# Seven products for one more channel matmul, features moved to ScalarE and an earlier load

One core of one Trainium2 chip runs the whole program. The metric is the device time of one execution in microseconds (us). All runs compared below are fast, at a granted TensorE clock of 0.99 to 1.00 (0.985 to 0.991 in e4), unless a sentence says otherwise. "The kernel before" and "the changed kernel" are the two kernels; batch b's attention and token mixing run inside the channel MLP of an earlier batch.

## The reference

```python
def phi(x, c, s):                     # c, s: cos and sin of pi/2 * position / 576
    r = np.maximum(x, 0.0)
    return np.concatenate([r * c, r * s], axis=-1)
q_p, k_p = phi(q, cos_w, sin_w), phi(k, cos_w, sin_w)      # q, k, v: 8 x 8 x 576 x 64
kv  = np.einsum('bhsf,bhsd->bhfd', k_p, v)
num = np.einsum('bhsf,bhfd->bhsd', q_p, kv)
den = np.einsum('bhsf,bhf->bhs', q_p, k_p.sum(axis=2))[..., None] + 1e-06
x = (num / den)                       # -> 8 x 576 x 512
h = np.maximum(x.T @ w_tok1, 0.0) @ w_tok2                 # token mixing, per batch
u = x + h.T
out = u + np.maximum(u @ w_ch1, 0.0) @ w_ch2               # channel MLP, 512 -> 1536 -> 512
```

## The kernel before

The program is a list of groups. Group g does the channel MLP of batch g in 12 steps of the first matmul and then the second matmul; each step also carries pieces of two later batches: numerators and token mixing of batch g+1 (`b` below), features, query transposes and KV sums of batch g+2 (`f`). From group 2 on the second matmul is done in seven products (a Strassen scheme: sums of the left operand on VectorE, seven quarter products on TensorE, sums of the results on VectorE and GpSimd). Group 1 is still the plain product, because its helpers had not found room.

Names used below: `h1T` is the relu of the first channel matmul, `B` the relu between the two token-mixing matmuls, `qpT` the transposed query features and `uT` the transposed u. A batch has 576 = 4.5 x 128 rows; its last 64 are its tail, and the tails of two batches are worked on together.

```python
def mlp2(g, t, part, ps, sub=(0, 4)):            # plain: 48 matmuls of 512 columns in group 1
    for ki in range(4 * part + sub[0], 4 * part + sub[1]):
        nc.tensor.matmul(ps, h1T[:, ki, t * P:(t + 1) * P], wc2[:, ki, :],
                         start=(ki == 0), stop=(ki == NCH - 1))
# ... in the seven-product form: 14 units of six matmuls of 256 columns
#     (products in order: A11*B11, S2*T2, S3*T3, S1*T1, A12*B21, A22*T4, S4*B22)

if g == 1:                                        # what group 1 carries, by step
    put(19, tail_turn, 1)                         # transpose of two batches' tail rows
    # ... KV and numerators of batch 2
    for j in range(NJ):
        put(8 + j, f1k, f, j, 1, A)               # batch 3: sine feature of k on ScalarE
        put(10 + j, f1k, f, j, 0, V)              #          cosine feature on VectorE
        put(8 + j, vcast, f, j, G)                #          cast of v on GpSimd
        put(18 + j, kv_step, f, j)
    for j, at in enumerate((12, 15, 16, 17, 18)):
        put(at, q_step, f, j)                     # q: cosine on VectorE, sine on ScalarE,
                                                  # then a DMA transpose qp -> qpT
    for i in range(4):
        put(19 + i, t_sum, i)                     # sums of the second weight
    put(8, v_load, 4); put(20, q_load, 4); put(22, k_load, 4)
# ... groups 2 to 6:
for j in range(NJ):
    put(2 + j, num_step, b, j)                    # numerators read qpT: group 2 reads batch 3's
```

In the groups shown here all loads and all DMA transposes are issued from SyncE, in program order; the outputs are stored from GpSimd. The loads of batch 3 (k, v, q) stood behind the five query transposes of batch 2.

## Time and profile before

The median was 262.94 us of 3 runs (262.86 to 263.52), the profiled span 261.9 us.

| stage | length, us | what TensorE waited for in it, us |
|---|---|---|
| group 1 (plain product) | 29.23 | 0.16 for a feature of k |
| group 2 | 27.78 | 0.34 and 0.27 for relus of h1T on ScalarE; 0.15 at its end for a transposed u |
| group 3 | 26.03 | none over 0.12 |
| groups 4 and 5 | 26.50, 25.86 | none over 0.12 |

A stage runs from the first matmul of one group to that of the next, so whatever delays it in between is in its length. The table is worked out from the starts of the groups' first matmuls (58.10, 87.33, 115.11, 141.14, 167.64 and 193.50 us). Groups 2 and 4 have the same instructions, so 26.50 us is what group 2 takes when nothing waits. One view that the prediction does not show matters later: TensorE in the middle of group 2, where it reads the transposed queries. (Columns of a timeline: start, length, engine, line, operation, out<-in, shape, count, and in brackets the idle time before it with what ended it.)

```profile
93.24 0.41 PE L207 MATMUL psA<-kv_sb,qpT 128*128 128x65 bf16 x8
94.35 0.41 PE L207 MATMUL psA<-kv_sb,qpT 128*128 128x65 bf16 x8
```

These are the fourth and fifth numerators of batch 3. No bracket: their transposes had landed at 90.14 and 91.43 us, 3.1 and 2.9 us early.

### The profile page before, as it was taken

The numbers are of one execution on the slowest core, as the hardware profiler recorded it, in microseconds if no ns is written. First come the engines' busy times: TensorE is split into PE (matmuls) and PEld (weight loads), VectorE is DVE, ScalarE is ACT, GpSimd is POOL, SyncE is SP. The second block draws the span as 40 slices with busy tenths as digits, with TensorE's granted clock in tenths as the row PEclk, the third lists the DMA queues.
The fourth block names the chain that finished last, engine by engine and source line by source line (L and its number), as shares of the span: only waits on it lengthen the run. The fifth ranks groups of instructions, "written<-read, shape, count | busy, mean of one in ns | idle before, by whom it ended". The sixth has DMA issues, their size and how long they took to land.

```text
span 261.9 us, 5595 instructions
## 1 busy us (share of the span) xinstructions
PE 250.9 (96%) x2060; PEld 154.4 (59%) x2074; DVE 187.2 (71%) x447; ACT 148.3 (57%) x246; POOL 97.9 (37%) x175
## 2 busy tenths in 40 slices
PE   7788999999999999999999999999999999999994
PEld 2465455554545554775587557755875576486483
DVE  5794657697959688948993999489939773563563
ACT  4664486785577438836792679367935452613610
POOL 5178465361042420292029402830291045045041
PEclk9999999999999999999999999999999999999999
DMA  6999999999987999989999997995381034003004
GB/s 188 356 371 388 391 388 387 326 180 267 379 270 159 251 298 357 221 188 305 361 193 179 323 343 151 185 290 99 65 215 70 3 80 161 19 3 150 13 0 161
DMA packets 79947, 57.18 MB, mean 218 GB/s; under 512 B 48176, under 2 KB 74928, under 8 KB 79920
## 3 DMA queue, kind: packets, MB, share of 16 engines
q1 hardware_dynamic: 76128, 47.26, 67.5%
q0 software_dynamic: 2560, 8.39, 9.3%
q10 hardware_dynamic: 1232, 1.18, 1.4%
q8 instruction: 16, 0.26, 0.4%
q14 instruction: 11, 0.09, 0.1%
HBM read 35.85 MB, written 9.44 MB: 173 GB/s over the span
## 4 chain that ended last, share of the span: by engine, by line
PE 54%; DMA 1%; ACT 1%; DVE 1%; issue 1%
PE psM L312 24%; PE psM L374 21%; PE psA L232 3%; PE psA L250 3%; PE psA L207 2%; PE psA L183 1%; DMA uT<-u_bf 1%; PE psA L374 1%; ACT kp L138 0%; PE psA L291 0%; ACT u_bt L299 0%; DVE res L397 0%; DVE res L423 0%; DVE qp L140 0%; DVE kp L140 0%
## 5 line engine op out<-in xcount | busy, mean ns | idle before, releaser
L312 PE MATMUL psM<-uT,w_ch 128*128 128x512 bf16 x368 | 88.0, 379 | 0.2
L324 ACT ACTIVATE h1T<-psM 128x512 bf16<-128x512 f32 x93 | 55.4, 597 | 42.3 <-PE psM L312 40.4
L312 PEld LDWEIGHTS <-w_ch 128*128 128x128 bf16 x416 | 38.1, 97 | 40.4 <-issue 0.4
L392 POOL TENSOR_TENSOR res<-res,u_sb 128x256 f32<-128x256 f32 x36 | 26.7, 772 | 78.2 <-DVE res L397 77.8
L156 POOL CAST vb<-v_raw 128x512 bf16<-128x512 f32 (+1 forms) x43 | 23.4, 589 | 25.2 <-DMA v_raw<-in_v_dram 12.3
L138 ACT ACTIVATE kp<-k_raw,sin_t 128x512 bf16<-128x512 f32 (+1 forms) x45 | 28.1, 666 | 1.2 <-DMA k_raw<-in_k_dram 1.2
L138 ACT ACTIVATE qp<-q_raw,sin_t 128x512 bf16<-128x512 f32 (+1 forms) x40 | 26.3, 681 | 4.4 <-DMA q_raw<-in_q_dram 4.4
L374 PEld LDWEIGHTS <-h1T 128*128 128x128 bf16 x252 | 23.8, 98 | 6.2 <-issue 0.6
L374 PEld LDWEIGHTS <-k_raw 128*128 128x128 bf16 x252 | 24.4, 98 | 5.1 <-issue 1.2
L330 PE MATMUL psM<-w_ch,h1T 128*128 128x512 bf16 x92 | 23.3, 379 | 0.2
L374 PE MATMUL psM<-w_ch,h1T 128*128 128x256 bf16 x168 | 22.3, 273 | 0.6 <-ACT h1T L324 0.6
L140 DVE TENSOR_SCALAR kp<-k_raw,cos_t 128x512 bf16<-128x512 f32 (+1 forms) x45 | 19.7, 465 | 1.8 <-DMA k_raw<-in_k_dram 1.8
L207 PEld LDWEIGHTS <-qpT 128*128 128x128 bf16 x320 | 14.9, 98 | 9.9 <-issue 1.8
L374 PE MATMUL psM<-w_ch_t,k_raw 128*128 128x256 bf16 x162 | 20.5, 273 | 0.0
L140 DVE TENSOR_SCALAR qp<-q_raw,cos_t 128x512 bf16<-128x512 f32 (+1 forms) x40 | 16.6, 447 | 5.4 <-DMA q_raw<-in_q_dram 5.2
L255 DVE TENSOR_TENSOR u_sb<-psA,x_sb 128x1024 f32<-128x1024 f32 x16 | 19.5, 1216 | 1.0 <-PE psA L250 0.8
L223 DVE TENSOR_TENSOR x_sb<-psA,rden 128x512 bf16<-128x512 f32 x28 | 19.4, 691 | 1.0
L354 DVE TENSOR_TENSOR k_raw<-h1T 128x512 bf16<-128x512 bf16 (+1 forms) x28 | 9.9, 353 | 11.8 <-ACT h1T L324 11.1
L250 PE MATMUL psA<-B,w_tok 128*128 128x512 bf16 x64 | 16.4, 379 | 0.0
L440 POOL DMA_DIRECT2D out_dram<-res x16 | 9.0, 560 | 18.6 <-DVE res L335 12.8
L219 DVE TENSOR_SCALAR rden<-psA 128x8 f32<-128x8 f32 x35 | 5.7, 163 | 13.4 <-PE psA L207 13.1
L193 ACT CAST kv_sb<-psA 128x520 bf16<-128x520 f32 x7 | 4.2, 603 | 18.9 <-PE psA L183 18.9
(134 smaller groups left out, 377.4 us busy)
## 6 DMA issues: line engine op xcount, KB each, us to landing
out_dram<-res POOLq DMA_DIRECT2D x32, 256.0 KB, 3.8
k_raw<-in_k_dram SPq DMA_DIRECT2D x7, 640.0 KB, 8.8
v_raw<-in_v_dram SPq DMA_DIRECT2D x7, 640.0 KB, 10.5
q_raw<-in_q_dram SPq DMA_DIRECT2D x7, 640.0 KB, 10.9
k_raw<-in_k_dram SPq DMA_DIRECT2D x7, 512.0 KB, 7.1
v_raw<-in_v_dram SPq DMA_DIRECT2D x7, 512.0 KB, 10.4
q_raw<-in_q_dram SPq DMA_DIRECT2D x7, 512.0 KB, 10.1
u_sb<-in_moe_w_ch_dram SPq DMA_DIRECT2D x2, 1024.0 KB, 10.6
```

Of the source, the lines that this page charges most:

```text
L138: eng.activation(out_ap, in_ap, AF.Relu, bias=0.0, scale=s)
L140: eng.tensor_scalar(out_ap, in_ap, scalar1=s, scalar2=0.0, op0=ALU.mult, op1=ALU.max)
L156: eng.tensor_copy(out_ap, in_ap)
L207: nc.tensor.matmul(dst, w, kv_sb[:, h, 0:E1], start=True, stop=True, skip_group_check=True)
L223: nc.vector.tensor_mul(dst.rearrange("p (g h d) -> p g h d", g=2, h=HH), n[:, :, :, 0:D], rb)
L250: nc.tensor.matmul(ps[:, half, :], w2[:, ki, 2 * c + half, :], B1[b % 2][:, ki, :], start=(ki == 0), stop=(ki == NT - 1))
L255: nc.vector.tensor_add(u_sb[b % 2][:, 2 * c:2 * c + 2, :], ps, x_sb[:, 2 * c:2 * c + 2, :])
L312: nc.tensor.matmul(ps.rearrange("p (t k) -> p t k", k=P), wc1[:, ki, mi * P:(mi + 1) * P], src[:, :, ki, :], start=(ki == 0), stop=(ki == ...
L324: eng.activation(h1T[:, mi, :], ps, AF.Relu)
L330: nc.tensor.matmul(ps, h1T[:, ki, t * P:(t + 1) * P], wc2[:, ki, :], start=(ki == 0), stop=(ki == NCH - 1))
L374: nc.tensor.matmul(m[tt][:, tt, :], a[:, c, tt * P:(tt + 1) * P], w[:, c, :], start=(pr < 4 and c == 0 and (tt == 0 or own)), stop=(c == N ...
L392: G.tensor_add(c[:, t, :], s[:, t, :], u[:, t, :])
```

## The change

Its intent: give group 1 the seven-product form as well (less TensorE work), and make room on VectorE by moving features of batch 3 to ScalarE. The values of batch 3 are loaded ahead of its keys, the weight sums are spread over group 1, and three of the four sums of group 1 live in the raw buffers of batch 2 (one of them in its q buffer, into which q of batch 4 is loaded later), since those of batch 3 are still in use.

```diff
+    S_of = {1: (rows_of(raw["k"][0], 0), rows_of(raw["k"][0], 1), rows_of(raw["q"][0], 0), S4_sb)}
@@ between the second and third query transpose of batch 2
+    load(3, v, "v", (SY, SY))
     for j in range(2, NJ):
         qfeat(2, j, A, A)
         qturn_dma(2, j)
+    for n in "kq":
+        load(3, src_of[n], n, (SY, SY))
@@ later
-    for n in "kvq":
-        load(3, src_of[n], n, (SY, SY))
@@ group 1's plan
+            for i, at in enumerate((4, 12, 17)):
+                put(at, t_sum, (1, 3, 2)[i])
+            put(10, s_sums, g, 0, 3)
+            put(11, s_sums, g, 3, 5)
-                put(8 + j, f1k, f, j, 1, A)
-                put(10 + j, f1k, f, j, 0, V)
-            for j, at in enumerate((12, 15, 16, 17, 18)):
-                put(at, q_step, f, j)
+                put((9, 10, 10, 11, 11)[j], f1k, f, j, 1, A)
+                put((12, 13, 18, 20, 21)[j], qfeat, f, j, (A, A, A, A, V)[j], A)
+                put((12, 13, 18, 20, 21)[j], qturn_dma, f, j)
+                put((15, 15, 17, 18, 19)[j], f1k, f, j, 0, (A, A, A, V, V)[j])
+                put(5, vcast, f, j, G)
-            put(20, q_load, 4)
+            put(22, q_load, 4)
@@ later groups
-            put(0, q_load, f + 1)
+            put(8 if g == 2 else 0, q_load, f + 1)
@@ the loop over the steps
-            elif g == 1:            # plain product
-                ...
-                mlp2(g, t, part, mps[t])
             else:
                 mlp2_unit(g, s - NCH)
                 mlp2_sums(g, s - NCH)
```

Cut: buffer views, arguments, the order of the first matmul's blocks in group 1, the first weight sum ahead of group 1, the lines that the new ones for `vcast`, `t_sum` and `kv_step` replace, and the transposes of u, which move two steps later in group 1.

## The prediction

> **What bounds the kernel now.** I read the page's busy shares and 40 slices first, then the chain of waits, then a table of windows with one stage per row, then the timelines of the engines inside the two stages that the change touches. Group g is batch g's channel MLP (g = 8: the tails of all batches); one stage is one group's first matmul (L312) and second matmul (L330, or L374 for the seven-product form), with the next batches' attention and token mixing woven in.
>
> ```profile
> PE 250.9 (96%) x2060; PEld 154.4 (59%) x2074; DVE 187.2 (71%) x447; ACT 148.3 (57%) x246; POOL 97.9 (37%) x175
> PE   7788999999999999999999999999999999999994
> PEclk9999999999999999999999999999999999999999
> ```
>
> TensorE is busy 250.9 of 261.9 us at the full granted clock. Only 11 us are idle, and slices 1 to 4 and the last, the head and the final store, hold most of them. So time comes off almost only by taking TensorE work away, or from the little idle time of a middle stage.
>
> ```profile
> 218.95 10.36 PE psM L312 x48
> 229.31 9.17 PE psM L374 x84
> ```
>
> These two lines of the chain of waits, near its end, give the real price of each kind of matmul where nothing disturbs it: 48 of 512 columns take 10.36 us, so 215.8 ns each; 84 of 256 columns take 9.17 us, so 109.2 ns each. (The groups' means of 379 and 273 ns contain the overlapping drains and must not be multiplied.)
>
> ```profile
> 58.10:87.33 29.23, 28.91 (x236) 14.75 (x238) 23.73 (x45) 17.27 (x29) 6.06 (x11) 1.00 0.92 266
> 87.33:115.11 27.78, 26.96 (x235) 17.14 (x235) 22.28 (x53) 16.48 (x28) 9.57 (x15) 1.00 1.12 269
> 115.11:141.14 26.03, 25.96 (x230) 17.18 (x232) 20.47 (x51) 16.69 (x27) 9.40 (x16) 1.00 1.11 258
> 141.14:167.81 26.67, 26.62 (x234) 17.26 (x236) 21.56 (x52) 17.26 (x28) 11.20 (x18) 1.00 1.02 249
> ```
>
> The windows are groups 1, 2, 3 and 4; columns: length, then busy us of PE, weight load, DVE, ACT, POOL, then clock, DMA share, GB/s. Group 1 is the last that still uses the plain second matmul. Group 2 does the same work as group 4 (both close a batch pair, with four tail matmuls) but lasts 27.78 against 26.67 us: 1.11 us of waiting. Where it waits:
>
> ```profile
> 101.58 0.71 PE L374 MATMUL psM<-w_ch,h1T 128*128 128x256 bf16 x5 [0.34 <-ACT h1T L324]
> 102.56 0.28 PE L374 MATMUL psM<-w_ch,h1T 128*128 128x256 bf16 x1 [0.27 <-ACT h1T L324]
> ```
>
> ```profile
> 98.74 0.72 ACT L138 ACTIVATE qp<-q_raw,sin_t 128x512 bf16<-128x512 f32 x1 [3.59 <-DMA q_raw<-in_q_dram]
> ```
>
> ```profile
> 111.98 2.99 DMA uT<-u_bf
> 114.97 0.14 issue
> 115.11 2.75 PE psM L312 x12
> ```
>
> ScalarE stood 3.59 us for q of batch 4; the relus queued behind it then hold TensorE for 0.34 + 0.27 us, and the whole backlog makes the transposed u of group 3 land at 114.97, so TensorE ends the stage with about 0.3 us more idle (its last product-and-KV work is done at about 114.8).
>
> **What the Trainium skill says.** "TensorE: Matmul & The Clock Gate", section Back-to-back issue gap, tabulates 262 cycles for 256 columns and 518 for 512 at 2.4 GHz: 109.2 and 215.8 ns, which is what the trace shows to the digit. The same section's sustained 131 ns for 512 columns is not seen here; the measurement decides. "SBUF — State Buffer", section Who interferes with whom, says that a VectorE instruction with two SBUF inputs, or in a two-port mode, and a GpSimd instruction that reads SBUF shut each other out for a whole instruction. The trace agrees: two sums of equal size, the second beside a cast on GpSimd:
>
> ```profile
> 82.86 0.95 DVE L341 TENSOR_TENSOR w_ch_t<-w_ch 128x1536 bf16<-128x1536 bf16 x1
> 83.84 1.53 DVE L343 TENSOR_TENSOR w_ch_t<-w_ch,w_ch_t 128x1536 bf16<-128x1536 bf16 x1
> ```
>
> ```profile
> 83.93 0.62 POOL L156 CAST vb<-v_raw 128x512 bf16<-128x512 f32 x1
> ```
>
> 1.53 - 0.95 = 0.58 us, nearly the cast's 0.62. "DMA: Bandwidth & Descriptors", section Queues, rings and completion order, says each DMA engine consumes a ring's descriptors in order. The loads of this kernel behave so: k, v and q of batch 3, issued in that order from 58.0 us, land at 66.8, 72.1 and 75.4 us. So the order in the program decides who waits.
>
> **The change, part by part.**
>
> 1. Group 1's second matmul: 48 x 215.8 ns = 10.36 us becomes 14 units x 6 x 109.2 ns = 9.17 us. Saved on the bounding engine: 1.19 us. A weight load (98 ns by the page) still hides under 109 ns.
>
> 2. What feeds it, on VectorE: sums of h1 (4 x three pieces) and, no longer after the stage but spread over it, the four weight sums. From the stage of group 2, four operations cost 1.46 us for two chunks (95.84 to about 97.6, less the blocked 0.31) and 1.0 us for one; three chunks scale to about 1.95. Together 1.95 + 1.46 + 1.0 = 4.4 us. The six bank sums of 0.6 replace four: +1.2. Away go four q and three k features at about 0.4 us pace: -2.8. Net about +2.8 us on 23.73 busy of 29.23: it fits on average. The first weight sum goes into a gap of 1.54 us before 51.96; the second (0.95 to 1.53) into this gap:
>
> ```profile
> 65.63 0.69 DVE L296 TENSOR_TENSOR u_tl<-psA,x_tc 128x512 f32<-128x512 f32 x1 [2.06 <-issue]
> ```
>
> The tight place is the third product, whose left operand is a sum over all chunks. TensorE reaches it at 74.03 + 2 x 0.655 + 0.86 = 76.2 us (start of the second matmul, two units, one u product). VectorE is free of the x outputs at 71.4; 1.95 + 0.6 (a relu) + 1.46 brings 75.4, and the second sum of the last chunk about 76.0. So the margin is about 0.2 us, 0 to 0.5 us may be lost.
>
> 3. ScalarE gets seven features at 0.61 us pace (+4.3) and a bank copy (+0.5): 17.27 becomes about 22 of 28 us. Walking its queue from the last relu at 75.2: two q features, copy, two more, u cast (waits for u_out at 78.6), two k features, u cast to 81.7, k, q, tail cast, q, q: done at about 85.8. The u transposes then land at about 84.8, before the stage's end near 86.1; each k feature is ready ahead of its KV step. It fits by little.
>
> 4. Loads. v of batch 3 is issued at about 52 instead of 59.5 us, so its five casts on GpSimd move from 72 to about 61 to 65 us, beside k features and the second weight sum; by the lock above each meeting costs VectorE up to 0.6 us. The gap of 2.06 us takes most of it; I count 0.3 us on TensorE.
>
> 5. q of batch 5 is put behind v of batch 5, and batch 4's q is free to go as soon as the q transposes of batch 3 are issued, at about 88.4 instead of 90.4. It then lands near 96.5 instead of 98.7, while the work before it ends 1.2 us earlier: ScalarE still waits, some 2.6 us instead of 3.59. TensorE would reach the first unit at 100.05; the relu that it needs is done at about 96.5 + 3.8 = 100.3 and is used by the sixth matmul only, 0.55 us later. So the 0.61 us vanish, and with a smaller backlog and fewer loads between, about half of the 0.5 us that group 2 loses elsewhere. I count 0.7.
>
> Stages from group 3 on have the same instructions; only where the sums lie is new. Sum: -1.19 (part 1) + 0.3 (third product) + 0.3 (lock) - 0.2 (small waits of group 1, which idles 0.3 us) - 0.7 (group 2) = about -1.5 us: 262.94 - 1.5 = 261.4 us.
>
> **The rivals.** (a) VectorE becomes group 1's bound: its share there was 81% already and the sums are in line with the third product. For: the margin of 0.2 us and the lock. Against: 2.06 us of gap and the features moved away. It would eat 0.6 to 1.2 us more: 262 to 262.6. (b) ScalarE becomes the bound: a late batch 3 q, or the u casts behind features, hold the u transposes and group 2 begins late. For: no slack is planned after 75 us. Against: q of batch 3 lands at 75.4 even today and is used from 75.2. It would give back 0.5 to 1 us, and 262.3. (c) Everything falls well: 1.19 + 0.3 + 1.1 = 2.6 us, 260.3; nothing more can be had, since the stages after it hardly idle (25.96 busy of 26.03). (d) The q load is hidden as before because the transposes in front of it move later with ScalarE's features: then part 5 gives 0.2 at most and the time is 261.9.
>
> **Range and chances.** The floor is (c); (a) and (b) together would nearly cancel the gain. 260.4 to 262.6 us should hold it 8 times in 10. Faster by over 2% needs 257.7 us, more than twice the largest gain found: 1%. Slower by over 2% needs a stall of 6.5 us: 1%. Within 2%: 98%.
>
> **What would show it right or wrong.** Part 1: the second matmul's lines at L330 lose 48 records and L374 gains 84; group 1's window shrinks from 29.23 to about 28.4. Part 2: an idle of TensorE before a product that reads the sums in k_raw, around 76 us, above 0.5 us means rival (a). Part 3: TensorE idle at the start of group 2, around 86 us, released by the u transpose, means (b). Part 4: the second weight sum takes 1.5 rather than 0.95 us. Part 5: the wait of ScalarE for q_raw near 94 us is under 3 us and the two TensorE waits for h1T are gone; group 2 lasts about 27.1. A gain elsewhere than in groups 1 and 2, or a stage from group 3 on that differs by over 0.2 us, would make the reading wrong.

## The result

The changed kernel took 265.36 us (median of 4 runs, 264.69 to 265.61) beside 262.9 us for the kernel before in the same rounds. The ratio is 1.0088, 95% interval 1.006 to 1.0117. Ratios here and below are the mean time of one kernel's fast runs over the mean of the other's fast runs in the same rounds, so they are not quite the ratios of the medians. So the change made the kernel slower by 0.9%: outside the predicted range, though still inside the class "within 2%".

First the page of the changed kernel, to be read against the one that the prediction shows of before:

```profile
PE 251.6 (96%) x2110; PEld 157.8 (60%) x2110; DVE 192.2 (73%) x454; ACT 152.7 (58%) x254; POOL 104.7 (40%) x181
```

TensorE's share is as before (its clock too, 1.00 in the windows below), and no other engine is full over the whole span. The page cannot show where the time went; the stages can. The windows of groups 1 and 2 of the changed kernel (length, then busy us of PE, weight load, DVE, ACT, POOL, then clock, DMA share, GB/s):

```profile
57.73:86.38 28.65, 28.05 (x276) 18.25 (x275) 26.33 (x50) 20.97 (x36) 10.36 (x14) 1.00 0.97 254
86.38:115.95 29.57, 27.19 (x240) 16.92 (x237) 22.52 (x54) 17.30 (x29) 10.90 (x18) 1.00 1.06 271
```

Group 1, the one that was changed, is 0.58 us shorter. Group 2, whose matmuls did not change, went from 27.78 to 29.57 us: +1.79. Group 3 is 0.18 shorter (25.85), group 4 as before, group 5 0.56 longer (26.42), the head before group 1 0.37 shorter; with these the span of 263.1 against 261.9 us adds up (-0.37 - 0.58 + 1.79 - 0.18 + 0.56 = 1.22).

The medians differ by 2.46 us, more than the 1.2 us of the two traces. About 0.7 of the rest is that the profiled run of before, 263.65 us, was above its median. And 0.3 us lie outside the recorded span: time less span is 1.8 us in the runs of the kernel before and 2.1 in those of the changed one. What those 0.3 us are stays open: some experiments with the seven products have 1.8 too, so it is not the products as such.

Where group 2 waits. TensorE in the changed kernel:

```profile
93.37 0.42 PE L212 MATMUL psA<-kv_sb,qpT 128*128 128x65 bf16 x8 [0.93 <-DMA qpT<-qp]
...
95.63 0.42 PE L212 MATMUL psA<-kv_sb,qpT 128*128 128x65 bf16 x8 [0.98 <-DMA qpT<-qp]
...
102.73 0.71 PE L380 MATMUL psM<-w_ch,h1T 128*128 128x256 bf16 x5 [0.21 <-ACT h1T L329]
103.71 0.28 PE L380 MATMUL psM<-w_ch,h1T 128*128 128x256 bf16 x1 [0.27 <-ACT h1T L329]
```

The fourth and fifth numerators, which waited for nothing before, now wait 0.93 and 0.98 us for their transposes; the waits for h1T are still there. Together 2.39 us against 0.76 before (0.34, 0.27 and 0.15): a difference of 1.63, nearly all of group 2's +1.79.

Why the transposes are late: SyncE's queue, before and changed. (Its length is the time that the queue takes to send the work, not to land it.)

```profile
82.30 6.72 SPq L162 DMA_TRANSPOSE qpT<-qp  x4
89.11 1.23 SPq L300 DMA_TRANSPOSE uTt<-u_bt  x1
90.39 2.04 SPq L132 DMA_DIRECT2D q_raw<-in_q_dram  x2
```

```profile
86.16 1.20 SPq L305 DMA_TRANSPOSE uTt<-u_bt  x1
87.45 3.92 SPq L167 DMA_TRANSPOSE qpT<-qp  x2
91.46 2.57 SPq L137 DMA_DIRECT2D q_raw<-in_q_dram  x2
```

Before, all four late query transposes went out by 89.0 us, ahead of the tail's. Now the tail's transpose stands in front of the last two, as the plan has it, and they go out at 87.45 and 89.50 and, by the trace's landing times, land at 93.33 and 95.58: 5.9 and 6.1 us later, where before they took 4.3 and 3.7. Behind them q of batch 4 goes out 1.1 us later and lands at 99.79 instead of 98.63. That is why ScalarE's wait for it did not shrink:

```profile
71.12 0.72 ACT L143 ACTIVATE kp<-k_raw,sin_t 128x512 bf16<-128x512 f32 x1 [1.90 <-DMA k_raw<-in_k_dram]
...
85.42 1.33 ACT L143 ACTIVATE qp<-q_raw,sin_t 128x512 bf16<-128x512 f32 x2
...
99.89 0.72 ACT L143 ACTIVATE qp<-q_raw,sin_t 128x512 bf16<-128x512 f32 x1 [4.55 <-DMA q_raw<-in_q_dram]
```

This timeline of ScalarE also shows the start of the delay. ScalarE stands 1.90 us for the keys of batch 3, which land at 71.02 us, behind the values, instead of 66.83. From 71.12 us it has no gap over 0.2 us until its last query feature ends at 86.75. And GpSimd, at just this moment:

```profile
81.10 5.27 POOL L398 TENSOR_TENSOR res<-res,u_sb 128x256 f32<-128x256 f32 x6 [15.61 <-DVE res L403]
87.81 0.56 POOL L446 DMA_DIRECT2D out_dram<-res  x1 [1.44 <-DVE res L422]
...
89.44 0.54 POOL L447 DMA_DIRECT2D out_dram<-res  x1
```

The seven-product form finishes all its outputs at the end of the stage, so its four stores go out together, among the last two transposes. The plain form had sent two at 82.8 and two at 88.6 us.

### The profile page after: what moved, and what is told of

Read it like the earlier page. It is cut to its first block, busy times and chain, and to the rows that moved or that the text cites. A ratio compares the mean times of both kernels' runs of the same rounds, so it can differ in the third digit from the quotient of the medians.

```text
span 263.1 us, 5706 instructions
## 1 busy us (share of the span) xinstructions
PE 251.6 (96%) x2110; PEld 157.8 (60%) x2110; DVE 192.2 (73%) x454; ACT 152.7 (58%) x254; POOL 104.7 (40%) x181
## 4 chain that ended last, share of the span: by engine, by line
PE 56%; DMA 2%; ACT 1%; DVE 0%; issue 0%
PE psM L317 24%; PE psM L380 21%; PE psA L237 3%; PE psA L255 3%; DMA uT<-u_bf 2%; PE psA L212 2%; PE psA L188 1%; ACT u_bf L265 1%; PE psA L296 1%; PE psA L380 1%; ACT kp L143 0%; DVE res L429 0%; DVE u_sb L260 0%
## 5 line engine op out<-in xcount | busy, mean ns | idle before, releaser
L398 POOL TENSOR_TENSOR res<-res,u_sb 128x256 f32<-128x256 f32 x42 | 31.9, 789 | 93.4 <-DVE res L403 93.0
L380 PEld LDWEIGHTS <-h1T 128*128 128x128 bf16 x288 | 27.1, 98 | 6.6 <-ACT h1T L329 0.6
L380 PE MATMUL psM<-w_ch,h1T 128*128 128x256 bf16 x192 | 25.4, 273 | 0.5 <-ACT h1T L329 0.5
L380 PE MATMUL psM<-w_ch_t,k_raw 128*128 128x256 bf16 x186 | 23.6, 273 | 0.0
L145 DVE TENSOR_SCALAR kp<-k_raw,cos_t 128x512 bf16<-128x512 f32 (+1 forms) x42 | 20.8, 522 | 1.8 <-DMA k_raw<-in_k_dram 1.8
L380 PEld LDWEIGHTS <-k_raw 128*128 128x128 bf16 x192 | 18.5, 98 | 4.9 <-issue 1.2
L359 DVE TENSOR_TENSOR k_raw<-h1T 128x512 bf16<-128x512 bf16 (+2 forms) x31 | 11.2, 361 | 12.8 <-ACT h1T L329 11.9
L145 DVE TENSOR_SCALAR qp<-q_raw,cos_t 128x512 bf16<-128x512 f32 (+1 forms) x36 | 15.5, 460 | 3.1 <-DMA q_raw<-in_q_dram 3.1
L212 PE MATMUL psA<-kv_sb,qpT 128*128 128x65 bf16 x280 | 14.3, 193 | 2.2 <-DMA qpT<-qp 1.9
L237 PE MATMUL psA<-x_sb,w_tok 128*128 128x512 bf16 x56 | 14.4, 379 | 0.2 <-DVE x_sb L228 0.2
```

The lines of the kernel that those rows point to most:

```text
L145: eng.tensor_scalar(out_ap, in_ap, scalar1=s, scalar2=0.0, op0=ALU.mult, op1=ALU.max)
L212: nc.tensor.matmul(dst, w, kv_sb[:, h, 0:E1], start=True, stop=True, skip_group_check=True)
L237: nc.tensor.matmul(b1_ps[b][mi], w1[:, jw, mi * P:(mi + 1) * P], x, start=(j == 0), stop=(j == T))
L380: nc.tensor.matmul(m[tt][:, tt, :], a[:, c, tt * P:(tt + 1) * P], w[:, c, :], start=(pr < 4 and c == 0 and (tt == 0 or own)), stop=(c == N ...
L398: G.tensor_add(c[:, t, :], s[:, t, :], u[:, t, :])
```

## The experiments

The theory after the result: the features on ScalarE and the order of the loads make the last query transposes of batch 3 late, into the burst of stores; TensorE waits for them, and the load of q behind them is late too. Rivals: the order of the loads alone does it; the late load of q alone sets group 2's end; the seven products themselves cost it (VectorE's sums); the stores alone do it. The runs correct the theory in one point, said at e11 and e2: the loads cost time, but not by making these transposes late. The expectations call theories by letters; what to compare is the number that each gives. All kernels below gave the right result. "Group 1" and "group 2" are stage lengths of the one profiled run of each kernel, in us; the fast runs of one kernel spread over 0.8 to 3.5 us, so tenths in these two columns are not to be compared without the wait behind them.

| run | kernel | fast runs: median us | ratio to before (95%) | group 1 | group 2 |
|---|---|---|---|---|---|
| – | before (profiled first) | 262.9 | 1 | 29.23 | 27.78 |
| – | changed | 265.36 | 1.0088 (1.006–1.0117) | 28.65 | 29.57 |
| e1 | changed, tail's transpose late | 265.14 | 1.0064 (1.0017–1.011) | 28.47 | 29.51 |
| e2 | changed, loads of batch 3 as before | 265.84 | 1.0092 (1.005–1.0133) | 29.09 | 30.46 |
| e3 | changed, cosine of q on VectorE | 265.84 | 1.0083 (1.0038–1.0127) | 32.11 | 29.00 |
| e4 | changed, four stores held back | 270.42 | 1.0265 (1.0214–1.0316) | 29.17 | 33.77 |
| e5 | changed, q of batch 4 early | 266.3 | 1.011 (1.0071–1.0148) | 29.39 | 31.10 |
| e6 | e5 with e1 | 265.02 | 1.0057 (1.002–1.0094) | 29.40 | 28.29 |
| e7 | before, q of batch 4 early | 263.7 | 1.0045 (1.0008–1.0081) | 29.23 | 27.93 |
| e8 | before with the products alone | 267.41 | 1.0185 (1.0152–1.0218) | 31.77 | 30.28 |
| e9 | e10 with q of batch 4 early | 264.14 | 1.0037 (1.0016–1.0058) | 30.38 | 26.51 |
| e10 | changed, keys first, transposes in time | 263.37 | 1.0002 (0.9982–1.0023) | 29.97 | 26.51 |
| e11 | before with the loads' order alone | 264.34 | 1.0045 (1.0018–1.0071) | 29.62 | 28.59 |
| e12 | before with the features alone | 264.53 | 1.0064 (1.0035–1.0093) | 29.23 | 30.43 |
| e13 | e10, values last | 262.99 | 1.001 (0.9979–1.0042) | 29.89 | 26.51 |
| e14 | changed, queries' order alone | 264.41 | 1.0053 (1.0017–1.0089) | 29.88 | 28.05 |
| e15 | e10, values first | 264.5 | 1.0094 (1.0056–1.0132) | 28.88 | 27.42 |

In e5, e6 and e15 one or two of the six runs counted as slow by their time (at clocks as in the others) and are left out of these medians; so is one run of the kernel before, of 530.7 us, in the rounds of e15. For e15 the recorded ratio is above what its fast runs as listed give (a mean of 264.72 over 262.68, so 1.008).

### The parts, one at a time

**e12: the kernel before with the features alone**

```diff
-                put(10 + j, f1k, f, j, 0, V)
+                put(10 + j, f1k, f, j, 0, (A, A, A, V, V)[j])
-                put(at, q_step, f, j)
+                put(at, qfeat, f, j, (A, A, A, A, V)[j], A)
+                put(at, qturn_dma, f, j)
```

> The kernel before with the move of features alone (four cosine q features and three cosine k features of batch 3 on ScalarE instead of VectorE). ScalarE gains 4.3 us of work in group 1, which has 17.3 of 29.2 us busy. If moving features is a cost by itself: the query transposes 3 and 4 of batch 3 are issued 1 to 3 us later than 85.8 and 87.8 us, TensorE waits for qpT in group 2 for 0.5 us or more, ratio 1.003 to 1.006. If it is harmless without the seven products: those waits stay away, group 2 at 27.8 us, ratio 0.999 to 1.002.

Without the products and with the old loads, the kernel before became 0.64% slower. TensorE in group 2:

```profile
95.08 0.42 PE L207 MATMUL psA<-kv_sb,qpT 128*128 128x65 bf16 x8 [0.68 <-DMA qpT<-qp]
...
102.48 1.02 PE L312 MATMUL psM<-uT,w_ch 128*128 128x512 bf16 x4 [1.36 <-ACT h1T L324]
104.06 0.71 PE L374 MATMUL psM<-w_ch,h1T 128*128 128x256 bf16 x5 [0.56 <-ACT h1T L324]
```

The same two waits as in the changed kernel: a numerator for its transpose (issued at 88.21, landed at 95.04), and relus queued behind q of batch 4, which ScalarE awaited for 6.18 us. So the features moved to ScalarE make group 2 wait by themselves. The profiled run was the slowest of its six (span 264.6; the others 262.4 to 263.6), so the size is to be taken from the ratio.

**e11: the kernel before with the loads' order alone**

```diff
+    load(3, v, "v", (SY, SY))
     (third to fifth query transpose of batch 2)
+    for n in "kq":
+        load(3, src_of[n], n, (SY, SY))
-    for n in "kvq":
-        load(3, src_of[n], n, (SY, SY))
-            put(20, q_load, 4)
+            put(22, q_load, 4)
-            put(0, q_load, f + 1)
+            put(8 if g == 2 else 0, q_load, f + 1)
```

> The kernel before with the changed order of loads alone (v of batch 3 early, k and q after the query transposes, q of batch 4 at step 22, q of batch 5 at step 8 of group 2). If the load order is itself a cost: the query transposes of batch 2 land 5 to 7 us later and k of batch 3 at about 71 us as in the changed kernel, ScalarE waits near 69 us and its queue is late to the end of group 1; the query transposes 3 and 4 of batch 3 come later; ratio 1.003 to 1.006. If it only matters together with ScalarE's added features: ScalarE has the room to catch up, group 1 stays at 29.2 us, group 2 at 27.5 to 27.9, ratio 0.999 to 1.002.

0.45% slower. Group 1 lost 0.39 us, and in group 2 the waits for h1T stayed (0.42 and 0.27) and one for a transposed u came to it:

```profile
115.31 1.46 PE L312 MATMUL psM<-uT,w_ch 128*128 128x512 bf16 x6 [0.90 <-DMA uT<-u_bf]
```

The query transposes were not what was late here: the last two landed at 89.67 and 91.15 us and TensorE did not wait for them.

In microseconds, 1.2 (e11) and 1.7 (e12) less the 1.19 that the products save make +1.7; the changed kernel measured about +2.3. Parts of one schedule need not add up; the size is of the same order.

**e8: the products alone** (loads of batch 3 and the engines of its features as before; sums, weight sums and the steps of all pieces as in the changed kernel)

```diff
-                put((12, 13, 18, 20, 21)[j], qfeat, f, j, (A, A, A, A, V)[j], A)
+                put((12, 13, 18, 20, 21)[j], qfeat, f, j, V, A)
-                put((15, 15, 17, 18, 19)[j], f1k, f, j, 0, (A, A, A, V, V)[j])
+                put((15, 15, 17, 18, 19)[j], f1k, f, j, 0, V)
     (and the three loads behind the transposes, k, v, q, and q of batch 5, as before)
```

> The seven products alone: the changed kernel with the three loads of batch 3 as in the kernel before, the load of batch 5's q at step 0 of group 2 again, and the cosine features of batch 3 on VectorE again. If the products are worth their 1.19 us by themselves: group 1 takes 28.0 us, ratio about 0.996. If VectorE cannot carry the features beside the sums, as the third experiment suggests (group 1 took 32.1 us there, with waits for B, v_raw and a bank): group 1 takes over 30 us and the ratio is 1.008 or more; then moving features to ScalarE was needed to make the products possible at all.

1.85% slower: group 1 took 31.77 us, with waits for the sums (0.72), a transposed u (1.01) and a bank not yet added (0.78), and group 2 still waited 1.12 and 0.64 us for the transposes, whose steps behind the tail's transpose were those of the changed kernel.

**e3: the changed kernel with the cosine of q on VectorE**

```diff
-                put((12, 13, 18, 20, 21)[j], qfeat, f, j, (A, A, A, A, V)[j], A)
+                put((12, 13, 18, 20, 21)[j], qfeat, f, j, V, A)
```

> The changed kernel with the four cosine q features of batch 3 back on VectorE (the sine ones stay on ScalarE). Theory F (ScalarE's added features make the q transposes late): ScalarE loses 4 x 0.61 = 2.4 us in group 1, the sine feature of the last tile ends 1.5 to 2.4 us earlier, the qpT waits fall under 0.7 us, ratio 1.002 to 1.005. Rival V (VectorE is no better: it is behind the bank sums, and each feature beside GpSimd's adds takes 1.0 instead of 0.48 us): the last cosine feature ends no earlier than 86.6 us, the qpT waits stay at 1.5 us or more, ratio 1.007 to 1.010.

Group 1 grew to 32.11 us, with waits up to 1.33 us, and the transposes still came 1.55 us late. So in this order of steps VectorE cannot carry these features beside the sums, and moving them, which is the intent of the change, was rightly seen as needed. Other orders with the features on VectorE were not tried.

**e2: the changed kernel with the loads of batch 3 as before**

```diff
-    load(3, v, "v", (SY, SY))
-    for n in "kq":
-        load(3, src_of[n], n, (SY, SY))
     (later, in front of group 1)
+    for n in "kvq":
+        load(3, src_of[n], n, (SY, SY))
```

> The changed kernel with the three loads of batch 3 back where and in the order in which the kernel before has them (k, v, q, after the q transposes of batch 2). Theory L (v's early load pushes the q transposes of batch 2 and so k of batch 3 back, from 58.0 to 63.7 us; ScalarE then waits 1.90 us for k and stays late to the end of group 1): k lands near 67 us, the wait of ScalarE for k_raw near 69 us is gone, TensorE's 0.44 us wait for B at 75.8 us is gone, and the qpT waits of group 2 shrink from 1.91 to about 1 us; ratio about 1.003 to 1.005. Rival: the backlog is caught up before the q features, then only the 0.44 us go and the ratio is 1.007.

No better than the changed kernel. The keys landed at 66.0 us, but now the casts of v met the first sums on VectorE (1.01, 0.96 and 0.96 us instead of 0.55), TensorE waited 0.80 us for the sums, and 1.83 us for the transposes. The last two transposes went out at 87.40 and 89.22 us, as in the changed kernel (87.45 and 89.50). So the order of the loads costs something by itself (e11), but it is not what makes these transposes late.

### Removing one wait uncovers the next

**e1: the tail's transpose behind the query transposes**

```diff
-            put(19, tail_turn, 1)
+            put(24, tail_turn, 1)
```

> The changed kernel with one edit: the cast and the transpose of the first pair's tail (needed only by group 8) are emitted in step 24 of group 1 instead of step 19, so behind the last query transposes and the loads of batch 4. Theory Q (the query transposes 3 and 4 of batch 3 come too late in the sync queue): without the tail's transpose in front, issued at 86.16 us and 1.2 us long, and with 0.5 us less on ScalarE, transposes 3 and 4 go out 1.0 to 1.8 us earlier and TensorE's two waits for qpT in group 2 (0.93 + 0.98 us) shrink to under 0.5 us in sum; ratio to the kernel before about 1.002 to 1.004 instead of 1.0088. Rival S (the burst of four stores at the end of group 1 slows the transposes): the waits stay near 1.9 us, ratio stays at 1.008.

SyncE's queue and TensorE of e1:

```profile
84.35 4.73 SPq L167 DMA_TRANSPOSE qpT<-qp  x3
89.19 2.60 SPq L137 DMA_DIRECT2D q_raw<-in_q_dram  x2
```

```profile
93.34 0.41 PE L212 MATMUL psA<-kv_sb,qpT 128*128 128x65 bf16 x8
...
99.92 1.02 PE L317 MATMUL psM<-uT,w_ch 128*128 128x512 bf16 x4 [0.56 <-ACT h1T L329]
101.50 0.71 PE L380 MATMUL psM<-w_ch,h1T 128*128 128x256 bf16 x5 [0.56 <-ACT h1T L329]
102.48 0.28 PE L380 MATMUL psM<-w_ch,h1T 128*128 128x256 bf16 x1 [0.27 <-ACT h1T L329]
```

The last two transposes went out at 86.09 and 87.44 us, 1.4 and 2.1 us earlier than in the changed kernel, by this one edit. Both waits for them are gone, as the theory says, and the time is nearly the same: q of batch 4 went out 2.3 us earlier but landed only 1.2 us earlier (98.56), so TensorE arrived early at the relus behind it and stood there instead; a wait of 0.94 us for a transposed u followed. In the kernel before, the changed one and e1, the end of the last wait for h1T follows the landing of q at the same distance: 98.63 and 102.56, 99.79 and 103.71, 98.56 and 102.48, that is 3.9 us each time. In these three kernels the load of q sets when the waits for h1T end, whatever is waited for ahead of them.

**e5: q of batch 4 loaded early; e6: the same with e1; e7: the same on the kernel before**

```diff
-    S_of = {1: (..., ..., rows_of(raw["q"][0], 0), S4_sb)}
+    S3_u = u_tl[:, 1:3, :]...                      # the third sum moves out of q's buffer
+    S_of = {1: (..., ..., S3_u, S4_sb)}
-            put(22, q_load, 4)
+            put(9, q_load, 4)
```

> The changed kernel; the third sum of group 1 lies in the unused part of the tail buffer instead of batch 2's q buffer, so that buffer is free, and the load of batch 4's q goes out at step 9 of group 1 (about 70 us) instead of step 22 (91 us). Theory D (group 2 ends when it does because q of batch 4 lands late: in the kernel before, the changed one and the first experiment, TensorE's second wait for h1T ended 3.9 us after that landing, whatever waited before it): q lands by 84 us, ScalarE's 4.55 us wait for q_raw and both h1T waits go, group 2 takes under 28.6 us instead of 29.6 even if the two qpT waits of 1.9 us stay; ratio about 1.000 to 1.004. Rival W (the late query transposes set the length of group 2): the waits for qpT stay and group 2 stays above 29.2 us, ratio 1.006 to 1.009.

> The same and, as in the first experiment, the cast and transpose of the first pair's tail behind the query transposes (step 24). Theory D with Q: no wait for qpT and none for h1T over 0.2 us, group 2 takes 26.7 to 27.3 us, group 1 about 28.5, span about 260.5 us: ratio 0.993 to 0.998, so faster than the kernel before. Rival: another transfer takes over as the bound (the u transposes of group 3): group 2 stays above 28.5 us.

> The kernel before with one edit: the load of batch 4's q goes out at step 9 of group 1 instead of step 20. Theory D says that the same load also costs the kernel before the 0.61 us of h1T waits and the late start of group 3: they go, group 2 takes 26.7 to 27.0 us instead of 27.8, ratio 0.995 to 0.998. Rival: in the kernel before the load is not the bound, group 2 stays at 27.8 us and the ratio at 1.000.

If the load of q alone set the end, e5 should have gained. It landed at 82.1 us and the waits for h1T are gone, but:

```profile
95.27 0.45 PE L213 MATMUL psA<-kv_sb,qpT 128*128 128x65 bf16 x8 [2.75 <-DMA qpT<-qp]
```

The fourth transpose, issued at 87.76, now landed at 95.22, 7.5 us later. e5 is no faster than the changed kernel (1.011 beside 1.0088, overlapping intervals); e6, with the tail's transpose out of the way, still waits 1.61 us for a transpose; and even the kernel before (e7) loses its h1T waits and gets one of 1.04 us for a transpose in their place. So there are two limits close behind one another, the transposes and the load of q, and taking away either shows the other.

**e4: the four stores of group 1 held back to the middle of group 2**

```diff
-                stores.append(lambda: store(g, 3, res[1]))
+                (held if g == 1 else stores).append(lambda: store(g, 3, res[1]))
     (the same for the other pair)
+            if g == 2 and s == 7:
+                stores += held
```

> The changed kernel with the four output stores of group 1 held back from the end of group 1 (87.8 to 89.4 us) to step 7 of group 2, so behind all q transposes of batch 3. Theory S (the burst of four stores lengthens the landing of transposes 3 and 4 from 3.1 to 5.9 and 6.1 us): they land within 3.5 us of issue, at about 91 and 93 us, both qpT waits vanish, ratio about 1.001 to 1.003. Rival Q (they are late at issue): landing shrinks by under 1 us, the waits stay above 1.2 us, ratio 1.006 to 1.009.

```profile
87.26 3.13 SPq L167 DMA_TRANSPOSE qpT<-qp  x2
90.49 1.31 SPq L137 DMA_DIRECT2D q_raw<-in_q_dram  x2
```

Issued at the same times as in the changed kernel, 87.26 and 89.12 us, the two transposes landed at 91.03 and 92.22 (3.8 and 3.1 us instead of 5.9 and 6.1), TensorE did not wait for them, and q landed at 96.83. So the stores slow the transposes. As a version it is useless: the held stores landed only at 104.73 us, group 2's first copy into their buffer began at 104.83, and TensorE stood 6.8 us at the start of group 3, so the total says nothing.

Most runs show the same pattern. A query transpose that was sent well before the stores landed 3.1 to 4.9 us later; one that was sent within half a microsecond of the first store, or among them, mostly took longer. The last two rows hold what does not fit:

| kernel | sent, us from the first store of the burst | landed after, us |
|---|---|---|
| before | 0.9 before | 3.7 |
| e10 | 3.7 and 2.3 before | 3.2, 3.1 |
| e1 | 1.7 before; 0.3 before | 3.7; 5.7 |
| e14 | 1.8 before; 0.4 before | 4.9; 5.1 |
| changed | 0.4 before; 1.7 after | 5.9; 6.1 |
| e5 | 0.2 after; 2.8 after | 7.5; 5.7 |
| e12 (two stores only) | 0.2 before | 6.8 |
| e2 | 0.4 before; 1.5 after | 4.8; 6.1 |
| e8 | 1.2 before; 1.6 after | 6.8; 6.0 |

The Trainium skill, "DMA: Bandwidth & Descriptors", section Queues, rings and completion order, says that each DMA engine takes turns between the queues that have work for it, a packet at a time. A transpose that shares the engines with stores of another queue would then land later, as here. It need not be stores: in e5 two transposes sent at 77.19 and 78.89 us, with no store near but the early load of q in flight until 82.13, took 5.8 us each. That two stores were enough in e12 is more than I can explain. Landing times also scatter for reasons that no run shows: three stores sent from 239 to 241.4 us took 2.5 to 2.9 us in the kernel before and 4.65 to 4.8 in the changed one, with no load or transpose in flight. The mechanism inside the queues was not tested.

### Getting the transposes out in time

**e14: only the order of the queries**

```diff
-                put((12, 13, 18, 20, 21)[j], qfeat, f, j, (A, A, A, A, V)[j], A)
-                put((12, 13, 18, 20, 21)[j], qturn_dma, f, j)
+                put((12, 13, 14, 17, 18)[j], qfeat, f, j, (A, A, A, A, V)[j], A)
+                put((12, 13, 14, 17, 18)[j], qturn_dma, f, j)
```

> The changed kernel with one edit: the q features of batch 3 and their transposes are emitted in steps 12, 13, 14, 17, 18 of group 1 instead of 12, 13, 18, 20, 21; loads, tail and all else as changed. If the transposes' place is what costs group 2 its time: transposes 3 and 4 are issued about 1 to 2 us earlier than 87.45 and 89.50 us, the qpT waits (1.91 us) fall under 0.6 us, q of batch 4 goes out and lands 1 to 2 us earlier, group 2 takes 27.0 to 28.6 us; ratio 1.001 to 1.006. If the late k of batch 3 keeps all of ScalarE's queue late: the waits stay at 1.2 us or more and the ratio at 1.007 to 1.010.

The transposes went out at 85.71 and 87.06 us, and the waits for them are gone (landed at 90.62 and 92.18), with the loads, the features' engines and the stores as in the changed kernel. But ScalarE, started late by the keys, is now late elsewhere: 1.20 us of waiting for B at 76.15 in group 1, and 1.05 us for h1T in group 2.

**e10: keys first, transposes in time; e9: with q of batch 4 early too**

```diff
-    load(3, v, "v", (SY, SY))              # between the transposes of batch 2
+    load(3, k, "k", (SY, SY))
-    for n in "kq":
+    for n in "qv":
-            put(19, tail_turn, 1)
+            put(24, tail_turn, 1)
-                put((9, 10, 10, 11, 11)[j], f1k, f, j, 1, A)
+                put(5 + j, f1k, f, j, 1, A)
     (queries as in e14)
-                put((15, 15, 17, 18, 19)[j], f1k, f, j, 0, (A, A, A, V, V)[j])
+                put((10, 10, 16, 18, 19)[j], f1k, f, j, 0, (A, A, A, V, V)[j])
```

> The same version without the early load of batch 4's q (third sum in batch 2's q buffer, q of batch 4 at step 22, as in the changed kernel). Theory D (once the query transposes are in time, q of batch 4 is the next bound): ScalarE waits for q_raw near 94 us, TensorE has h1T waits of 0.3 to 0.8 us 2.9 us after q lands, group 2 takes 27.3 to 28.5 us, 0.5 to 1.5 us more than with the early load; ratio 0.996 to 1.001. Rival: with the transposes out of the way q lands early enough; group 2 as short as with the early load.

> A version meant to beat both: the seven products of group 1 as changed, but k of batch 3 (not v) is the load that goes out early, so ScalarE makes the sine k features in steps 5 to 9, where it idles between relus; the q features and transposes of batch 3 go out in steps 12, 13, 14, 17, 18 instead of 12, 13, 18, 20, 21, so all are issued before the four stores at the end of group 1; the tail's transpose is behind them; the third sum lies in the tail buffer and q of batch 4 is loaded at step 9. If the late query transposes are what group 2 lost its time to: no wait for B, qpT or h1T over 0.2 us, group 1 under 28.4 us, group 2 26.7 to 27.3 us, span about 260 us, ratio 0.992 to 0.997. If another cost stays (casts of v at 75 to 79 us beside the sums on VectorE; the early q load slows transposes): group 1 over 28.8 us and ratio 1.000 or more.

Windows of groups 1 and 2 in e10, and its queue:

```profile
57.66:87.63 29.97, 28.16 (x274) 18.22 (x274) 27.92 (x52) 21.17 (x36) 10.08 (x13) 1.00 1.03 253
87.63:114.14 26.51, 26.46 (x239) 17.17 (x237) 21.59 (x52) 17.36 (x28) 11.15 (x18) 1.00 1.05 287
```

```profile
84.27 2.61 SPq L167 DMA_TRANSPOSE qpT<-qp  x2
86.97 1.30 SPq L137 DMA_DIRECT2D q_raw<-in_q_dram  x2
```

Group 2 is 26.51 us, as group 4, with no wait of TensorE at all: 3.06 us less than in the changed kernel. With keys early, ScalarE is done early, the transposes go out at 84.27 and 85.61, before the stores, and the load of q follows at once. So group 2's loss can be removed whole, with the products and the four stores kept; e10 makes four edits at once, and which of them does what is read from e1, e4 and e14. But the time only equals the kernel before, because group 1 now takes 29.97 us. TensorE and VectorE of e10 there:

```profile
77.72 0.28 PE L380 MATMUL psM<-w_ch_t,k_raw 128*128 128x256 bf16 x1 [1.25 <-DVE k_raw L360]
```

```profile
73.76 0.43 DVE L359 TENSOR_TENSOR k_raw<-h1T 128x512 bf16<-128x512 bf16 x1
74.22 0.71 DVE L360 TENSOR_TENSOR k_raw<-k_raw,h1T 128x512 bf16<-128x512 bf16 x1
74.86 0.82 DVE L361 TENSOR_TENSOR q_raw<-h1T 128x512 bf16<-128x512 bf16 x1
```

The values, now loaded last, are cast on GpSimd from 73.99 to 77.5 us. The sums of two chunks, 0.42 us each when alone, take 0.71 to 0.82 beside the casts, and the first product that reads the sums waits 1.25 us. e9 did not gain from the early load, since in e10 nothing in group 2 waits for it any more.

**e13: the values still later**

```diff
-    for n in "qv":
-        load(3, src_of[n], n, (SY, SY))
+    load(3, q, "q", (SY, SY))
     (in front of group 1)
+    for b in (4, 3):
+        load(b, v, "v", (SY, SY))
```

> The tenth experiment's kernel (k of batch 3 early, q features and transposes in steps 12 to 18, tail last) with v of batch 3 loaded behind v of batch 4 instead of before it: it lands near 78.5 instead of 73.8 us, so its five casts on GpSimd run after VectorE's sums of h1 and not beside them. If the meeting of casts and sums made group 1's 1.25 us wait for k_raw: the sums of two chunks take 0.42 us again instead of 0.71 to 0.82, that wait falls under 0.3 us, group 1 takes 28.2 to 28.8 instead of 29.97 us, group 2 stays at 26.5, span about 259.5 us, ratio 0.993 to 0.998. If the sums are late by themselves: the wait stays above 0.9 us and the ratio at 1.000.

The sums are back at 0.42 and the wait for them is gone. The fourth weight sum, which is written into the buffer of these values, waits for the casts in its turn (GpSimd to 81.42):

```profile
81.45 1.48 DVE L350 TENSOR_TENSOR v_raw<-w_ch,w_ch_t 128x1536 bf16<-128x1536 bf16 x1 [1.14 <-POOL vb L161]
```

TensorE waits 0.91 and 0.62 us for what follows, and the kernel again only equals the one before.

**e15: the values first of all**, in front of the query transposes of batch 2

```diff
     (e10)
+    load(3, v, "v", (SY, SY))
     for j in range(2):
         qfeat(2, j, A, A)
         qturn_dma(2, j)
-    for n in "qv":
-        load(3, src_of[n], n, (SY, SY))
+    load(3, q, "q", (SY, SY))
```

> Edit: the kernel of e10 (features of k first, query transposes of batch 3 in time), with v of batch 3 loaded in front of the query transposes of batch 2 instead of behind q. In e10 the values landed at 72.1 and 73.8 us, their casts on GpSimd (74.0 to 77.5) met the sums on VectorE, and TensorE waited 1.25 us for the third product's operand at 77.72; group 2 had no wait at all. Theory L (what is left of the loss in e10 is this meeting of casts and sums, so early values undo it, and the values can come early without holding back what the query transposes of batch 3 depend on): casts done before 66 us, sums 0.56 and less, the wait before the third product under 0.4 us, group 1 about 28.7, group 2 26.5 to 26.7, span about 259.4, ratio to the kernel before 0.993 to 0.997. Rival M (each place in the queue costs another): the query transposes of batch 2, now behind 2 x 1 MB of values, land after 64 us and TensorE waits for them in group 1, or k lands later than 61 and ScalarE's queue runs late again with waits of over 0.5 us in group 2: span 260.5 to 262.5, ratio 1.000 or above.

```profile
57.21:86.09 28.88, 28.15 (x275) 18.22 (x274) 26.73 (x52) 21.08 (x36) 10.23 (x13) 1.00 1.00 240
86.09:113.51 27.42, 26.98 (x240) 17.15 (x237) 21.98 (x52) 17.11 (x29) 11.22 (x18) 1.00 1.10 279
```

The meeting is gone and with it the wait: group 1 is at 28.88 us. But batch 2's last query transposes now land at 67.5 to 69.1 us, TensorE waits 0.57 us in the numerators (the view puts it to VectorE; it ends as the third transpose has landed, at 67.48), and batch 3's queries land at 73.61 instead of 70.57. Group 2 is longer than in e10 by 0.9 us. The profiled run was the fastest of its six; the other fast ones spread to 266.4, and the kernel is not shown to be faster than the changed one. The rival of this run (each place in the queue costs another) holds.

No version that I tried beats the kernel before: e10 and e13 equal it, with intervals that lie between 0.998 and 1.004.

## Why the prediction was wrong

**Part 1, the products: right in price.** In the changed kernel two units of group 1 start 1.31 us apart for 12 matmuls (78.61 to 79.92), 109.2 ns each; in the kernel before eight plain matmuls take 1.73 us (74.03 to 75.76), 216 ns each. With the listed waits taken out, group 1 went from 29.07 (29.23 - 0.16) to 28.05 us (28.65 - 0.16 - 0.44): 1.02 of the 1.19 us.

**Part 2, the sums: right, with some luck.** Three chunks took 0.55 us per sum, two 0.42, one 0.28, and the first product that reads them did not wait. That was close: the last chunk's sum ended at 76.87 us, and the sixth matmul of that product, which reads it, came at about 76.98 (76.44 + 5 x 0.109), after TensorE had stood 0.44 us for B. Without that wait it would have stood some 0.3 us here (an estimate from these times). Rival (a) did not come true in the changed kernel; in e2, e8, e9 and e10, where the casts or features lay otherwise, it did (0.80, 0.72, 1.23 and 1.25 us). What was missed here is a wait of 0.44 us for B, a relu queued on ScalarE behind the late features of k.

**Part 4, the lock: seen, but elsewhere.** The second weight sum took 0.94 us, not 1.5, although it ran beside the casts:

```profile
63.51 0.94 DVE L348 TENSOR_TENSOR w_ch_t<-w_ch,w_ch_t 128x1536 bf16<-128x1536 bf16 x1
```

```profile
62.28 3.20 POOL L161 CAST vb<-v_raw 128x512 bf16<-128x512 f32 x4 [0.50 <-PE psA L188]
```

Here GpSimd lost: 3.20 us for four casts of 0.61 (2.44) are 0.76 too many, nearly all of it in one cast of 1.29 us that began at 63.63. The Trainium skill's page "SBUF — State Buffer" says in the section Who interferes with whom that the order of issue decides who is held. This pair agrees (the sum began at 63.51, first); the pair that the prediction shows does not, since there the sum began at 83.84, 0.09 us before the cast, and was the one held. So the record does not settle who pays. VectorE paid at 82 to 86 us instead, beside GpSimd's additions: features of 0.96 and 1.04 us that take 0.47 when alone (60.41). The part's larger mistake was to look only at this lock. The early load of v also pushed the keys of batch 3 from 66.83 to 71.02 us and with them the start of ScalarE's work; the 0.44 us for B in group 1 fits that (0.23 with the loads alone in e11, none in e2, where the keys landed at 66.0).

**Part 3, "It fits by little": this is the step that failed.** ScalarE was done at 86.75 us against 85.8 said, a small miss. But the check that followed asked only for the u transposes and the features of k. Five query transposes hang on the same queue, and group 2 wants the last two at 92.44 (93.37 - 0.93) and, if the fourth had been there, about 93.5 us. Before they had landed 3.1 and 2.9 us before use. Now they go out behind the tail's transpose, at 87.45 and 89.50, among four stores, and land 5.9 and 6.1 us later: 0.9 and about 2 us too late. Neither the place behind the tail's transpose (steps 20 and 21 behind its 19), nor the burst of stores, nor the slower landing beside it was in the sum. One edit at a time shows the first (e1, e14) and the stores (e4): with either, the waits for the transposes are gone. "Fits" cost 1.91 us that stood nowhere.

**Part 5, the load of q: failed by the same step.** It was to go out at 88.4, as soon as the transposes in front of it had gone. The reasoning about the order was right and the time of the transposes was not: it went at 91.46 and landed at 99.79 (96.5 said). ScalarE waited 4.55 us (2.6 said; 3.59 before), and the waits for h1T stayed at 0.48 of 0.61 us. Group 2 was to win 0.7 and lost 1.79, which is 2.5 of the 2.7 us by which the two spans miss the predicted difference of -1.5. (A small misreading on the way: the prediction's window of group 4 ends at 167.81 us, but group 5 begins at 167.64, so group 2's loss against group 4 was 1.28 and not 1.11 us.)

**The rivals.** Rival (d) named the right thing, transposes that move later with ScalarE's features, and made of it only a gain not had (261.9). It did not ask what else waits for those transposes. Rival (b) saw a late ScalarE, but at the start of group 2 and through the u transposes: there was no wait there. The prediction said that a stage from group 3 on that differs by over 0.2 us would make the reading wrong: group 5 does, by 0.56, of which 0.40 is a wait for one transposed u that landed 5.2 us after it was sent at 189.43. Waits of 0.3 to 0.9 us at that place come in e1, e2, e6, e13, e14 and e15 too, and not in before, e3, e4, e5, e7, e8 and e10 to e12 (in e9 TensorE waited 0.61 us there, for a sum on VectorE); what decides it is open.

**What is shown and what is not.** Shown: the features on ScalarE alone cost 0.64% (e12, interval from 0.35%) and the loads alone 0.45% (e11, from 0.18%), the first with late transposes, the second without; the waits for the transposes go when these are sent earlier (e1, e14) or the stores are held back (e4); with the transposes and the load of q in time, group 2's whole loss is gone (e10, e13). Shown for the orders tried only: the products need the features off VectorE (e3, e8). Argued and not shown: how the stores and transposes get in each other's way. Not settled: whether a schedule exists that keeps the products' gain; five orders were tried and each gave it back in group 1 or group 2.

## What to carry to other kernels

When work moves to another engine, list everything that hangs on that engine's last result, follow each item through the queue that it shares to its landing time, and set that beside the time at which it is read: an item with 3 us of slack today is a bound tomorrow. A change in when results are finished also changes when they are stored, and here a burst of stores delayed the transfers beside it (e4). When two limits lie within a microsecond of each other, removing one shows only the other, so judge an experiment by its waits as well as by its time.

## What the Trainium skill lacked or had wrong

- "Advanced Engine Details and Errata", section X-Bar Transpose (TRN2), says that transposing DMAs are as fast as regular ones. Alone they nearly were (256 KB of queries landed after 3.0 to 3.3 us and 256 KB of u mostly after 2.7 us; plain stores of 256 KB from SyncE and ScalarE at the program's end after 2.1 to 2.5). Sent next to four stores of 256 KB each, they took 5.7 to 7.5 us and the stores 2.5 to 5.9 (changed kernel, e1, e5); the page does not speak of this case.
- "DMA: Bandwidth & Descriptors" has a table of cycles that transposes take in the issuing sequencer, but for "previous generations" beside trn3, with no clock and for other sizes. What a transpose of 256 KB costs the queue that issues it on this chip is not there: 1.23 us each here when nothing holds it, against about 0.63 for one of the plain loads, so three in a row delay what stands behind them by 3.7 us before it is sent.
- "SBUF — State Buffer", section Who interferes with whom, gives the rule of the lock and that the order of issue decides who waits. It gives no hint which side that is in a stream of both: VectorE paid 0.71 to 0.82 instead of 0.42 us in e10 (and GpSimd up to 0.81 instead of 0.61 us per cast), GpSimd 0.80 us per cast on average in the changed kernel. In the kernel before the instruction that began first was the one held (a sum of 1.53 us from 83.84, a cast of 0.62 from 83.93).
